# A Fourier mixing stage on one Trainium2 core: complex weights by three real products, transforms two steps ahead, inverses in one float32 pass

## The chip, the cores and the metric

The kernel runs on one core of a Trainium2 chip. The metric is the device time of one execution in microseconds (us); three executions of the kernel before took 1865.67, 1866.29 and 1866.52 us, median 1866.29. Lower is better.

## What is computed

Input `x` has 4 batches of 3072 rows and 256 columns. The reference transforms along the rows, mixes the 256 columns with a complex matrix, applies a soft threshold, transforms back, and feeds the result to two further blocks:

```
X = rfft(x, axis=1)
Yr = Xr @ w_r - Xi @ w_i + b_r
Yi = Xr @ w_i + Xi @ w_r + b_i
Y = soft_threshold(Yr, 0.01) + 1j * soft_threshold(Yi, 0.01)
y = irfft(Y)
x1 = moe(y)          # softplus/tanh gate between two matrices
out = moe2(x1)       # channel mix with a shift by one row
```

The change touches the first four lines and the inverse transform only. They are `part1` of the kernel, the first sixth of its time; `part2`, the two further blocks, is not touched.

## The kernel before, in words

`part1` splits the transform of length 3072 into small transforms of length 24, which VectorE does as additions and scaled additions on the tile `a` (4 MB, one per batch, two buffers), and products with 128x128 matrices, which TensorE does. The work is a loop `for u in range(48)`: 4 batches of 12 steps. `b, t = divmod(u, 12)`. Step u handles one residue class, in this order on TensorE:

- **F(u+1)**, `emit_F`: the forward transform of the next class, out of `a` and the plane `fm[t]`, into PSUM tile `xps`. It is a plain float32 product of 256 columns (4 products in the code, 8 matmul records in a trace).
- **M(u)**, `emit_M`: the complex mix into PSUM tile `yps`, which ScalarE has preloaded with the bias (`preload`). F's result is split by `post_F` into a rounded part `xh` (ScalarE copy to float32r) and a rest `xl` (VectorE subtraction), the weights into `wmh` and `wml`; three of the four products are taken. With [-wi | wr | wi] side by side in the weights, real and imaginary part each take one product of 512 columns: 3 terms x 2 halves of the contraction x 2 parts = 12 products of 512 columns. Steps with t = 0 hold two special rows and take 24 products of 256 columns.
- **I(u-1)**, `emit_I`: the inverse transform into PSUM tile `bps`. 13 steps do it as one plain float32 product with the plane `im`; the 35 steps in `SPLIT_I` do it as three products of float32r parts (`zh`, `zl` against the planes `imhi`, `imlo`), 12 products of 256 columns.

Around these, in the program order of the other engines: `post_M(u-1)` thresholds on ScalarE (`yb`), `post_I(u-2)` copies `bps` to `bs` and SyncE stores it to `b_dr`. VectorE's short transforms of later batches, and the length-24 back transforms `f3` on the tile `g`, are background work: a small planner (`Background`) keeps a clock of its own and fits them ahead of each `post_F` by the constants `SLACK` and by due steps.

Transfers run on queues that issue in order. SyncE's holds the loads of `a`, the stores to `b_dr` and `y_dr`, and the plain planes `im`. GpSimd's holds the split planes, and twice (u = 6 and u = 18) the helper `end_sum`, four calls (six transfers) that add thirds of `x` onto `a` in flight: the first pair waits for the load of lines 24 to 31, the second pair waits for the first. The planes go through a ring of 12 slots (`RING`, `stream`, `load_stream`), each 256 KB; a slot is refilled when the inverse that read it is done.

```
while sent < len(stream) and (sent < RING and u or sent >= RING and stream[sent - RING][0] <= u):
    load_stream(sent)
```

For batches 2 and 3 the tile `a` of two batches before is overwritten: lines 24 to 31 and 16 to 23 at t = 6, lines 8 to 15 and 0 to 7 at t = 10, each after the last F that reads them.

Of the kernel before, what the change touches and what calls it, by code (L numbers as in the profile page):

```python
# [11 lines left out]
F32 = mybir.dt.float32  # L12
F32R = mybir.dt.float32r
# [12 lines left out]
NB = 4  # L26
# [6 lines left out]
NT = 12  # L33
# [7 lines left out]
START = (18600, 20500)  # L41
SLACK = (2000, 3200, 600)

SUMS_AT = (11, 12, 23, 24)
LOWS_AT = 35
SPLIT_I = (*range(6, 10), *range(12, 22), *range(24, 34), *range(36, 47))
SPLIT_F = (45, 46)
TWO_PASS = range(42)
FIRST = tuple(u + 1 for u in SPLIT_I)
F3_PART1 = {(1, 2): [(0, 0)], (1, 8): [(0, 1)]}  # L50
# [129 lines left out]
def tile_fft_mix_moe_channel_mix(  # L180
# [30 lines left out]
    def tt(o, a, b, op):  # L211
        V.tensor_tensor(out=o, in0=a, in1=b, op=op)  # L212
# [4 lines left out]
    def act(o, i, f, **kw):  # L217
        S.activation(out=o, in_=i, func=f, **kw)  # L218
# [19 lines left out]
    def slot(dtype, name, k, i=None):  # L238
        if i is None:
            i = slots[0] % 24  # L240
            i += 8 * (8 <= i < 16) - 8 * (i >= 16)
            slots[0] += 1
            if i >= RING:
                i = RING + (i - RING + len(stream)) % RING
        return mat.tile([128, 512], dtype, tag="m%d" % (i % 24), name=name).rearrange("p (k f) -> p k f", k=k)

    RING = 12
    stream = []
# [24 lines left out]
    def priced(ops):  # L273
        return [(cost(256 * n), e) for op in ops for n, e in op]
# [417 lines left out]
    def part1():  # L692
        with ExitStack() as es:
# [18 lines left out]

            xt, ybt, ybs, xps, yps, bps, lows, flow, xsp, spare = {}, {}, {}, {}, {}, {}, {}, {}, {}, {}

# [33 lines left out]
            def post_F(u):  # L748
                t = u % NT
                ps = xps.pop(u)  # L750
                xh = xs_p.tile([128, 2, 256], F32R, tag="xh", name="xh")
                xl = xs_p.tile([128, 2, 256], F32R, tag="xl", name="xl")
                act(xh, ps, ACTF.Copy)
                tt(xl, ps, xh.bitcast(F32), SUB)
                xt[u] = (xh, xl)
                if t == 0:
                    zh, zl = (new_z(w).rearrange("p (h f) -> p h f", h=2) for w in ("zh", "zl"))
                    xt[u] += (zh, zl)
                    copy_z(u, 0)
                    if u == 0:  # L760
                        copy_z(u, 1)
# [7 lines left out]
            def preload(u):  # L769
                ps = yps[u] = psy.tile([128, 512], F32, tag="y", name="yps")  # L770
                act(ps, bias, ACTF.Copy)
                if u % NT == 0:
                    act(ps[0:1, 256:512], bias[0:1, 0:256], ACTF.Copy)

            def emit_M(u, part=None):
                t = u % NT
                ps = yps[u]
# [121 lines left out]
            for t in range(2, 4):  # L899
                nc.sync.dma_start(out=fm[t], in_=fsrc[:, t])  # L900
            for n in range(4):
# [3 lines left out]
            for n in range(4, SPLIT_I[0]):  # L905
                load_stream(n)
            sent = SPLIT_I[0]
            for i, v in enumerate((mu_k, mu_r)):
# [17 lines left out]
            bg.flush()  # L926
            m = split_mix(c1, mraw[0], 0) + split_mix(c1, mraw[1], 1)
            preload(0)
            post_F(0)
# [7 lines left out]
            bg.add(priced(tail[:7]), 5)  # L937
            bg.add(priced(tail[7:]), 8)
            NU = NB * NT
            mv[0] = ysrc = None  # L940
# [7 lines left out]
            pe, bg.clock = START  # L948
            x_at, y_at = bg.clock, 0.0
            for u in range(NU):  # L950
# [10 lines left out]
                if u == SUMS_AT[0] - 4:  # L961
# [12 lines left out]
                    emit(wq.load(u))  # L974
                bg.flush(u + 1)
                if u == 6:
                    S.activation(out=mu1, in_=mu, func=ACTF.Copy, scale=-1.0, bias=1.0)
                pe += (1450 if u + 1 in SPLIT_F else 1755) * (u + 1 < NU)
                if u + 1 < NU:
                    (emit_F3 if u + 1 in SPLIT_F else emit_F)(u + 1)  # L980
                if u:
# [31 lines left out]
                if u + 1 < NU:  # L1013
                    bg.until(pe + 700 + (0 if u == 0 else SLACK[2] if (u + 1) % NT == 0 else SLACK[1]) - sum(c for c, e in behind))
                    post_F(u + 1)
                    x_next = bg.spend(pe + 700, 602)
                if u >= SUMS_AT[0] - 3:
# [12 lines left out]
                pe = max(pe, x_at + 300) + (2720 if u else 900)  # L1030
                y_new = pe + 700
                if u:
                    emit_I(u - 1)
                    pe = max(pe, y_at + 300) + (1370 if u - 1 in SPLIT_I else 1755)
                x_at, y_at = x_next, y_new
# [571 lines left out]
```

## Time and profile before

| what | us or share |
|---|---|
| median of 3 runs | 1866.29 |
| profiled execution: its own time | 1866.71 |
| profiled execution: span from the first to the last instruction | 1864.9 |
| TensorE matmul busy | 1846.6 (99%) |
| TensorE weight load busy | 1596.3 (86%) |
| VectorE busy | 1404.7 (75%) |
| ScalarE busy | 1243.9 (67%) |
| mean granted TensorE clock | 0.997 |
| `part1` on TensorE: from the start to the last inverse | 0 to about 318 |

Shares are over the whole span. `part1` has its own limits, so it is read from its own stretch: which engine waits there, for what, and how long one step lasts on TensorE. A matmul's modelled end overlaps the next one's start, so the length of a group of products is taken from its start to the start of the next group.

### The profile page before, as it was taken

How to read it: one execution, taken by the hardware profiler on the slowest of the kernel's cores; microseconds unless marked ns; L12 is line 12 of the kernel's file. 1: busy time of each engine (PE TensorE's matmuls, PEld its weight loads, DVE VectorE, ACT ScalarE, POOL GpSimd, SP SyncE). 2: the span in 40 equal slices, each digit the busy share in tenths (PEclk: the TensorE clock that was granted, in tenths of full speed). 3: DMA queues.
4: the chain of work that ended last, by engine and by line, in shares of the span. 5: the costliest groups of instructions: out<-in, count | busy, mean ns of one | idle time of the engine just before them, and what ended most of it. 6: DMA issues, size and time to landing. Idle time of an engine off the chain costs nothing.

```text
span 1864.9 us, 27267 instructions
## 1 busy us (share of the span) xinstructions
PE 1846.6 (99%) x9798; PEld 1596.3 (86%) x9798; DVE 1404.7 (75%) x2494; ACT 1243.9 (67%) x2231; POOL 60.9 (3%) x103
## 2 busy tenths in 40 slices
PE   9998999999999999999999999999999999999999
PEld 7887888888888888888888888888999999999998
DVE  8896957998798879597777867666676666666654
ACT  4655588665667657575766757576877777777775
POOL 1212110000000000000000000000000000000000
PEclk9999999999999999999999999999999999999999
DMA  9969697545656554555646455452422222222211
GB/s 321 239 200 295 167 291 263 182 150 167 197 166 196 156 166 145 172 155 156 197 131 194 151 165 170 125 189 85 153 68 69 68 69 69 69 69 69 69 46 34
DMA packets 191509, 281.77 MB, mean 151 GB/s; under 512 B 17040, under 2 KB 106896, under 8 KB 191120
## 3 DMA queue, kind: packets, MB, share of 16 engines
q1 hardware_dynamic: 175360, 255.39, 43.3%
q0 software_dynamic: 14944, 23.60, 5.1%
q8 instruction: 78, 1.28, 0.3%
q10 hardware_dynamic: 1072, 1.05, 0.2%
q14 instruction: 55, 0.45, 0.1%
HBM read 203.43 MB, written 76.55 MB: 150 GB/s over the span
## 4 chain that ended last, share of the span: by engine, by line
PE 93%; DVE 3%; DMA 2%; issue 1%; SPq 0%; ACT 0%; POOL 0%; DVEq 0%; POOLq 0%; ACTq 0%
PE a L221 28%; PE x L221 16%; PE v L221 14%; PE c L221 11%; PE z L221 5%; PE d L221 5%; PE yps L221 5%; PE zps L221 4%; PE xps L221 3%; PE bps L221 3%; DMA a<-in_x_dram 1%; DMA y_dr<-g 1%; DVE a L212 1%; DVE g L212 1%; DMA imlo<-in_sel_dram 0%
## 5 line engine op out<-in xcount | busy, mean ns | idle before, releaser
L212 DVE TENSOR_TENSOR l<-k,h 128x512 fp32r<-128x512 f32 x576 | 391.7, 688 | 304.8 <-ACT k L218 150.6
L221 PE MATMUL a<-h,wo 128*128 128x512 f32 x1536 | 520.9, 389 | 0.0
L221 PEld LDWEIGHTS a<-h,wo 128*128 128x128 f32 x1536 | 288.3, 188 | 60.2
L221 PE MATMUL a<-l,wo 128*128 128x512 f32 x768 | 298.8, 389 | 0.0
L221 PE MATMUL v<-wv,h 128*128 128x256 f32 x1536 | 274.4, 278 | 0.0
L221 PEld LDWEIGHTS v<-wv,h 128*128 128x128 f32 x1536 | 244.4, 188 | 13.7
L218 ACT ACTIVATE k<-c 128x512 f32<-128x512 f32 x288 | 172.8, 600 | 108.4 <-PE c L221 96.2
L221 PE MATMUL x<-yc,wr 128*128 128x512 f32 x864 | 243.2, 390 | 0.0
L218 ACT ACTIVATE c<-x 128x512 f32<-128x512 f32 x288 | 169.5, 589 | 88.9 <-PE x L221 74.3
L218 ACT ACTIVATE k<-k 128x512 f32<-128x512 f32 x288 | 178.1, 633 | 65.9 <-DVE k L212 63.6
L221 PE MATMUL v<-wv,l 128*128 128x256 f32 x768 | 213.0, 277 | 0.0
L221 PEld LDWEIGHTS x<-yc,wr 128*128 128x128 f32 x864 | 161.9, 188 | 34.5 <-ACT d L218 0.4
L218 ACT ACTIVATE d<-x 128x512 f32<-128x512 f32 x144 | 84.6, 587 | 145.9 <-PE x L221 144.9
L221 PEld LDWEIGHTS a<-l,wo 128*128 128x128 f32 x768 | 144.1, 188 | 29.8
L221 PE MATMUL c<-yc,wr 128*128 128x512 f32 x576 | 161.8, 389 | 0.0
L221 PEld LDWEIGHTS v<-wv,l 128*128 128x128 f32 x768 | 144.4, 188 | 0.0
L218 ACT ACTIVATE h<-k 128x512 fp32r<-128x512 f32 x192 | 118.6, 629 | 30.2 <-DVE k L215 28.2
L212 DVE TENSOR_TENSOR k<-d,zs 128x512 f32<-128x512 f32 x144 | 98.8, 686 | 42.5 <-PE d L221 42.2
L221 PEld LDWEIGHTS c<-yc,wr 128*128 128x128 f32 x576 | 108.1, 188 | 22.6
L212 DVE TENSOR_TENSOR yc<-src,yc 128x512 fp32r<-128x512 f32 x168 | 112.0, 686 | 14.3 <-ACT yc L218 13.8
L221 PE MATMUL x<-yc,wk 128*128 128x512 f32 x432 | 122.5, 392 | 0.0
L212 DVE TENSOR_TENSOR g<-g 128x128 f32<-128x128 f32 (+3 forms) x264 | 111.1, 442 | 0.8
(122 smaller groups left out, 2896.5 us busy)
## 6 DMA issues: line engine op xcount, KB each, us to landing
wr<-h_dr SPq DMA_DIRECT2D x288, 256.0 KB, 2.7
b_dr<-bs SPq DMA_DIRECT2D x48, 256.0 KB, 4.6
src<-y_dr SPq DMA_DIRECT2D x24, 512.0 KB, 4.1
wr<-h_dr SPq DMA_DIRECT2D x96, 128.0 KB, 2.1
xk_dr<-tm SPq DMA_DIRECT2D x48, 256.0 KB, 3.1
xr_dr<-tm SPq DMA_DIRECT2D x48, 256.0 KB, 3.2
xr<-xr_dr SPq DMA_DIRECT2D x24, 512.0 KB, 3.8
src<-xk_dr SPq DMA_DIRECT2D x24, 512.0 KB, 4.3
```

The source lines that it names most:

```text
L212: V.tensor_tensor(out=o, in0=a, in1=b, op=op)
L218: S.activation(out=o, in_=i, func=f, **kw)
L221: T.matmul(out=o, lhsT=l, rhs=r, start=start, stop=stop, **kw)
```

## The change

It does five things.

1. **Three real products** for the 36 steps u = 9 to 47 with t > 0 (`gauss`). `post_F` also forms the sum of real and imaginary part (`xsf`: a ScalarE copy and a VectorE addition, both 128x256) and splits it (`xs`: one ScalarE copy, one VectorE subtraction). **G1(u+1)**, `emit_G1`, runs in step u: 6 products of 256 columns of that shared sum with wr, into one half of `yps`. `copy_G` has ScalarE copy this half into the other, in PSUM. **G2(u)**, `emit_G2`, then adds 13 products of 256 columns: one that adds the difference of the biases (`bo`), 12 with the weights wi - wr and -(wr + wi) (`wg`), which VectorE and ScalarE prepare once (`gauss_w`, `gauss_b`, due by step 9). `preload` copies 256 bias columns where it copied 512.
2. **All inverses plain**: `SPLIT_I` and `SPLIT_F` are empty. The planes `imhi`, `imlo`, `fmhi`, `fmlo` and the parts `zh`, `zl` of Y fall away.
3. **F two steps ahead** from step 8 on; step 7 does F(8) and F(9). Every third `xh`, `xl` pair lies in two former ring slots.
4. **The ring has 3 slots** and only `im` planes; from the fourth on they are issued by GpSimd. 10 plain planes that SyncE loaded move there.
5. The overwrite of `a` at t = 6 moves to t = 5 in batch 1, the one at t = 10 to t = 9 in both batches; the planner's costs and `SLACK` get new numbers.

```
-SLACK = (2000, 3200, 600)
+SLACK = (2000, 3200, 600, 1500)
+T_F, T_M, T_G1, T_G2, T_I = 1600, 2860, 730, 1690, 1725
-SPLIT_I = (*range(6, 10), *range(12, 22), *range(24, 34), *range(36, 47))
-SPLIT_F = (45, 46)
+SPLIT_I = ()
+SPLIT_F = ()
-FIRST = tuple(u + 1 for u in SPLIT_I)
+LEAD = 7
+FIRST = range(LEAD, NB * NT)
-    RING = 12
+    RING = (14, 16, 17)
...
+            gauss = lambda u: u > LEAD + 1 and u % NT
...
+                if gauss(u):
+                    act(xsf, ps[:, :, 0:128], ACTF.Copy)
+                    tt(xsf, ps[:, :, 128:256], xsf, ADD)
                 act(xh, ps, ACTF.Copy)
                 tt(xl, ps, xh.bitcast(F32), SUB)
                 xt[u] = (xh, xl)
+                if gauss(u):
+                    z = mat.tile([128, 512], F32R, tag="m%d" % (22 if u % 2 else 15), name="xs").rearrange(
+                        "p (s h f) -> p s h f", s=2, h=2)
+                    sh, sl = xsum[u] = z[:, 0], z[:, 1]
+                    act(sh, xsf, ACTF.Copy)
+                    tt(sl, xsf, sh.bitcast(F32), SUB)
...
+            def emit_G1(u):
+                ps = yps[u]
+                sh, sl = xsum.pop(u)
+                for k, (z, lo) in enumerate(((sh, 0), (sh, 1), (sl, 0))):
+                    for h in range(2):
+                        mm(ps[:, 0:256], z[:, h], wt["mix", h][lo][:, 256:512], False, k == 2 and h == 1, skip_group_check=True)
+
+            def copy_G(u):
+                act(yps[u][:, 256:512], yps[u][:, 0:256], ACTF.Copy)
+
+            def emit_G2(u):
+                ps = yps[u]
+                xs = xt.pop(u)
+                mm(ps[:, 256:512], ones, brow, False, False, skip_group_check=True)
+                for k, (zl, lo) in enumerate(((0, 0), (0, 1), (1, 0))):
+                    for h in range(2):
+                        for r in range(2):
+                            mm(ps[:, 256 - 256 * r:512 - 256 * r], xs[zl][:, h, 128 * r:128 * r + 128],
+                               wt["gauss", h][lo][:, 256 * r:256 * r + 256], False, k == 2 and h == 1, skip_group_check=True)
...
-                z = slot(F32 if kind == "im" else F32R, kind, 2, RING + n % RING)
+                z = slot(F32 if kind == "im" else F32R, kind, 2, RING[n % len(RING)])
-                    nc.sync.dma_start(out=z, in_=isrc[:, t])
+                    (nc.gpsimd if n >= len(RING) else nc.sync).dma_start(out=z, in_=isrc[:, t])
...
+                ahead = [v for v in ([u + 1] if u < LEAD else [u + 1, u + 2] if u == LEAD else [u + 2]) if v < NU]
...
+                if u + 1 < NU and gauss(u + 1):
+                    emit_G1(u + 1)
+                    copy_G(u + 1)
+                    pe = max(pe, x_at[u + 1] + 300) + T_G1
                 emit_M(u, None if u else 1)
...
-                if t == NT - 6 and b + 2 < NB:
+                if t == NT - 6 - b and b + 2 < NB:
...
-                if t == NT - 2 and b + 2 < NB:
+                if t == NT - 3 and b + 2 < NB:
...
-                while sent < len(stream) and (sent < RING and u or sent >= RING and stream[sent - RING][0] <= u):
+                while sent < len(stream) and stream[sent - len(RING)][0] <= u:
```

On TensorE, one step of batch 1 reads so before (`xps` is F, `yps` M, `bps` I; x4 counts the products of the code):

```order
L221 MATMUL xps<-fm,a 128x256 x4
L221 MATMUL yps<-wmh_261,xh 128x512 x2
L221 MATMUL yps<-wmh_266,xh 128x512 x2
L221 MATMUL yps<-wml_262,xh 128x512 x2
L221 MATMUL yps<-wml_267,xh 128x512 x2
L221 MATMUL yps<-wmh_261,xl 128x512 x2
L221 MATMUL yps<-wmh_266,xl 128x512 x2
L221 MATMUL bps<-imhi,zh 128x256 x4
L221 MATMUL bps<-imlo,zh 128x256 x4
L221 MATMUL bps<-imhi,zl 128x256 x4
```

and so in the change:

```order
L223 MATMUL xps<-fm,a 128x256 x4
L223 MATMUL yps<-wmh_255,xs 128x256
L223 MATMUL yps<-wmh_260,xs 128x256
L223 MATMUL yps<-wml_256,xs 128x256
L223 MATMUL yps<-wml_261,xs 128x256
L223 MATMUL yps<-wmh_255,xs 128x256
L223 MATMUL yps<-wmh_260,xs 128x256
L223 MATMUL yps<-bo 128x256
L223 MATMUL yps<-wg,xh 128x256 x8
L223 MATMUL yps<-wg,xl 128x256 x4
L223 MATMUL bps<-im,yb 128x256 x4
```

Twelve products of 512 columns became 6 + 13 of 256, and the six (G1) belong to the next step; the twelve products of the inverse became the four of the plain one.

On GpSimd's queue, around the first `end_sum` (the rows `a`), before; the plane `imlo_609` right behind it is read by I(12):

```order
L842 DMA imlo_422<-in_sel_dram 128x512
L842 DMA imhi_555<-in_sel_dram 128x512
L362 DMA a_165<-in_x_dram 128x4x256
L362 DMA a_165<-in_x_dram 128x2x256 x2
L362 DMA a_165<-in_x_dram 128x3x256
L362 DMA a_165<-in_x_dram 128x256
L362 DMA a_165<-in_x_dram 128x4x256
L842 DMA imlo_609<-in_sel_dram 128x512
```

and in the change, where `im_554` is the plane of I(7):

```order
L877 DMA im_554<-in_inv_dram 128x512
L362 DMA a_165<-in_x_dram 128x4x256
L362 DMA a_165<-in_x_dram 128x2x256 x2
L362 DMA a_165<-in_x_dram 128x3x256
L362 DMA a_165<-in_x_dram 128x256
L362 DMA a_165<-in_x_dram 128x4x256
L877 DMA im_606<-in_inv_dram 128x512
L877 DMA im_670<-in_inv_dram 128x512
```

The plane behind `end_sum` is now that of I(8), which TensorE reaches in step 9. At the second `end_sum` it is the plane of I(19), which TensorE reaches in step 20, three steps after the loads of that `end_sum` are issued.

On SyncE's queue, the overwrite of lines 8 to 15 and 0 to 7 of batch 0's tile stands so before:

```order
L612 DMA raw_695<-in_moe_w_in_dram 128x2x256 x2
L878 DMA b_dr0_57<-bs_740 128x2x256
L878 DMA b_dr0_57<-bs_802 128x2x256
L362 DMA a_165<-in_x_dram 128x6x256
L362 DMA a_165<-in_x_dram 128x2x256
L362 DMA a_165<-in_x_dram 128x4x256 x2
L878 DMA b_dr0_57<-bs_872 128x2x256
```

and so in the change:

```order
L612 DMA raw_695<-in_moe_w_in_dram 128x2x256 x2
L915 DMA b_dr0_57<-bs_734 128x2x256
L362 DMA a_165<-in_x_dram 128x6x256
L362 DMA a_165<-in_x_dram 128x2x256
L362 DMA a_165<-in_x_dram 128x4x256 x2
L915 DMA b_dr0_57<-bs_796 128x2x256
```

The four loads stand one store, that is one step, earlier.

## Rows read from the trace of the kernel before

**Rows 1.** Windows of the trace: us, then busy time of PE, PEld, DVE, ACT, POOL, clock, DMA.

```profile
100.00:150.00 50.00, 47.99 (x251) 41.76 (x252) 49.31 (x98) 26.65 (x47) 11.12 (x15) 0.97 0.72 201
...
266.00:272.00 6.00, 6.00 (x35) 5.27 (x33) 5.01 (x11) 5.91 (x12) 1.06 (x2) 1.00 1.00 318
```

**Rows 2.** Timeline of PE, one undisturbed step: start, us, instruction.

```profile
200.86 1.28 PE L221 MATMUL yps<-wmh,xh 128*128 128x512 f32 x4
...
203.81 0.64 PE L221 MATMUL bps<-imhi,zh 128*128 128x256 f32 x4
...
205.24 1.89 PE L221 MATMUL xps<-fm,a 128*128 128x256 f32 x8
```

**Rows 3.** Timeline of PE, the step with t = 0 and a plain inverse.

```profile
90.85 0.47 PE L221 MATMUL yps<-wmh,xh 128*128 128x256 f32 x1
...
93.91 1.89 PE L221 MATMUL bps<-im,yb 128*128 128x256 f32 x8
95.64 1.89 PE L221 MATMUL xps<-fm,a 128*128 128x256 f32 x8
```

**Rows 4.** Timeline of PE, a step whose F is split too.

```profile
294.00 0.64 PE L221 MATMUL xps<-fmhi,yc 128*128 128x256 f32 x4
...
295.44 1.09 PE L221 MATMUL yps<-wmh,xh 128*128 128x512 f32 x4
...
298.19 0.64 PE L221 MATMUL bps<-imhi,zh 128*128 128x256 f32 x4
```

**Rows 5.** Timeline of PE, steps 13 and 14, with what ended the idle time.

```profile
97.18 1.28 PE L221 MATMUL yps<-wmh,xh 128*128 128x512 f32 x4
...
104.11 0.75 PE L221 MATMUL bps<-imhi,zl 128*128 128x256 f32 x4 [2.01 <-DVE zl L212]
...
113.79 1.28 PE L221 MATMUL yps<-wmh,xh 128*128 128x512 f32 x4
```

**Rows 6.** Timeline of PE, step 25.

```profile
171.38 1.89 PE L221 MATMUL xps<-fm,a 128*128 128x256 f32 x8
...
182.35 2.07 PE L221 MATMUL yps<-wmh,xl 128*128 128x512 f32 x4 [6.90 <-DVE xl L212]
...
188.98 1.28 PE L221 MATMUL yps<-wmh,xh 128*128 128x512 f32 x4
```

**Rows 7.** Timeline of DVE ahead of those two places.

```profile
92.75 2.36 DVE L212 TENSOR_TENSOR a<-a 128x1024 f32<-128x1024 f32 x2 [5.30 <-DMA a<-in_x_dram]
...
99.19 0.68 DVE L212 TENSOR_TENSOR xl<-xps,xh 128x512 fp32r<-128x512 f32 x1
...
174.93 2.36 DVE L212 TENSOR_TENSOR a<-a 128x1024 f32<-128x1024 f32 x2 [2.32 <-DMA a<-in_x_dram]
```

**Rows 8.** Timeline of PE: F(7), F(8) and F(19).

```profile
54.06 1.89 PE L221 MATMUL xps<-fm,a 128*128 128x256 f32 x8
...
60.25 1.89 PE L221 MATMUL xps<-fm,a 128*128 128x256 f32 x8
...
130.03 1.89 PE L221 MATMUL xps<-fm,a 128*128 128x256 f32 x8
```

**Rows 9.** Timeline of POOL: the first plane behind each end_sum.

```profile
77.68 1.10 POOL L842 DMA_DIRECT2D imlo<-in_sel_dram  x1
...
149.76 1.10 POOL L842 DMA_DIRECT2D imhi<-in_sel_dram  x1
```

**Rows 10.** DMA view, the planes issued at 77.68 and 149.76: KB, us to landing.

```profile
imlo<-in_sel_dram POOLq DMA_DIRECT2D x1, 256.0 KB, 6.2
...
imhi<-in_sel_dram POOLq DMA_DIRECT2D x1, 256.0 KB, 11.0
```

**Rows 11.** Tile view of imhi, all 35 loads.

```profile
DMA to landing us min/median/max: 2.9/5.3/12.6
```

**Rows 12.** Timeline of ACT, two copies of 256 columns.

```profile
288.02 0.73 ACT L218 ACTIVATE wo<-q 128x256 fp32r<-128x256 f32 x2
288.64 0.60 ACT L218 ACTIVATE bs<-bps 128x512 f32<-128x512 f32 x1
```

More of the change, by code (lines that the diff above doesn't have):

```diff
@@ L242, in slot @@
             slots[0] += 1
-            if i >= RING:
-                i = RING + (i - RING + len(stream)) % RING
         return mat.tile([128, 512], dtype, tag="m%d" % (i % 24), name=name).rearrange("p (k f) -> p k f", k=k)
-    RING = 12
+    RING = (14, 16, 17)
     stream = []
@@ L711, in new_a @@
                 load_x(As[b], b)
-            xt, ybt, ybs, xps, yps, bps, lows, flow, xsp, spare = {}, {}, {}, {}, {}, {}, {}, {}, {}, {}
+            xt, xsum, ybt, ybs, xps, yps, bps, lows, flow, xsp, spare = {}, {}, {}, {}, {}, {}, {}, {}, {}, {}, {}
+            gauss = lambda u: u > LEAD + 1 and u % NT
             def emit_F(u):
@@ L750, in post_F @@
                 ps = xps.pop(u)
-                xh = xs_p.tile([128, 2, 256], F32R, tag="xh", name="xh")
-                xl = xs_p.tile([128, 2, 256], F32R, tag="xl", name="xl")
+                if u % 3:
+                    xh, xl = [xs_p.tile([128, 2, 256], F32R, tag=w, name=w) for w in ("xh", "xl")]
+                else:
+                    xh, xl = [slot(F32R, w, 2, i) for w, i in (("xh", 12), ("xl", 13))]
+                if gauss(u):
+                    act(xsf, ps[:, :, 0:128], ACTF.Copy)
+                    tt(xsf, ps[:, :, 128:256], xsf, ADD)
                 act(xh, ps, ACTF.Copy)
@@ L770, in preload @@
                 ps = yps[u] = psy.tile([128, 512], F32, tag="y", name="yps")
+                if gauss(u):
+                    act(ps[:, 0:256], bias[:, 0:256], ACTF.Copy)
+                    return
                 act(ps, bias, ACTF.Copy)
@@ L773, in preload @@
                     act(ps[0:1, 256:512], bias[0:1, 0:256], ACTF.Copy)
+            def emit_G1(u):
[15 more added lines that the diff above has]
+                               wt["gauss", h][lo][:, 256 * r:256 * r + 256], False, k == 2 and h == 1, skip_group_check=True)
             def emit_M(u, part=None):
+                if gauss(u):
+                    return emit_G2(u)
                 t = u % NT
@@ L900, in part1 @@
                 nc.sync.dma_start(out=fm[t], in_=fsrc[:, t])
-            for n in range(4):
+            for n in range(len(RING)):
                 load_stream(n)
@@ L904, in part1 @@
                 nc.sync.dma_start(out=fm[t], in_=fsrc[:, t])
-            for n in range(4, SPLIT_I[0]):
-                load_stream(n)
-            sent = SPLIT_I[0]
+            sent = len(RING)
             for i, v in enumerate((mu_k, mu_r)):
@@ L927, in part1, with gauss_w, low, gauss_b @@
             m = split_mix(c1, mraw[0], 0) + split_mix(c1, mraw[1], 1)
+            xsf = c1.tile([128, 2, 128], F32, name="xsf")
+            for h in range(2):
+                wt["gauss", h] = [mat.tile([128, 512], F32R, tag="m%d" % (18 + 2 * h + k), name="wg") for k in range(2)]
+            bo = mat.tile([128, 512], F32R, tag="m23", name="bo")
+            brow, ones = bo[:, 0:256], bo[:, 256:384]
+            def gauss_w(h):
+                q = pools["st"].tile([128, 512], F32, tag="q", name="q", bufs=3)
+                hi, lo = wt["gauss", h]
+                wr, wi = mraw[h][:, 0, :], mraw[h][:, 1, :]
+                def low():
+                    act(hi, q, ACTF.Copy)
+                    tt(lo, q, hi.bitcast(F32), SUB)
+                return [(420.0, lambda: tt(q[:, 0:256], wi, wr, SUB)),
+                        (420.0, lambda: stt(q[:, 256:512], wr, -1.0, wi, MULT, SUB)), (700.0, low)]
+            def gauss_b():
+                q = pools["st"].tile([128, 512], F32, tag="q", name="q", bufs=3)
+                def low():
+                    act(brow, q[:, 0:256], ACTF.Copy)
+                    act(ones, fm[1][:, 0, 0:128], ACTF.Copy, scale=0.0, bias=1.0 / 64)
+                    tt(brow[64:128], q[64:128, 0:256], brow[64:128].bitcast(F32), SUB)
+                return [(420.0, lambda: tt(q[:, 0:256], bias[:, 256:512], bias[:, 0:256], SUB)), (420.0, low)]
             preload(0)
@@ L938, in part1 @@
             bg.add(priced(tail[7:]), 8)
+            bg.add(gauss_w(0) + gauss_w(1) + gauss_b(), LEAD + 2)
             NU = NB * NT
@@ L948, in part1 @@
             pe, bg.clock = START
-            x_at, y_at = bg.clock, 0.0
+            x_at, y_at = {0: bg.clock}, 0.0
             for u in range(NU):
@@ L974, in part1 @@
                     emit(wq.load(u))
-                bg.flush(u + 1)
+                ahead = [v for v in ([u + 1] if u < LEAD else [u + 1, u + 2] if u == LEAD else [u + 2]) if v < NU]
+                bg.flush(max(ahead, default=u))
                 if u == 6:
                     S.activation(out=mu1, in_=mu, func=ACTF.Copy, scale=-1.0, bias=1.0)
-                pe += (1450 if u + 1 in SPLIT_F else 1755) * (u + 1 < NU)
-                if u + 1 < NU:
-                    (emit_F3 if u + 1 in SPLIT_F else emit_F)(u + 1)
+                f_end = []
+                for v in ahead:
+                    emit_F(v)
+                    pe += T_F
+                    f_end.append(pe)
                 if u:
@@ L1012, in part1 @@
                     behind = wq.vec(u, 4)
[L1013 to L1016, printed above, removed]
+                for v, e in zip(ahead, f_end):
+                    bg.until(e + 700 + (0 if u == 0 else SLACK[2] if v % NT == 0 else SLACK[3] if gauss(v) else SLACK[1]) - sum(c for c, e in behind))
+                    post_F(v)
+                    x_at[v] = bg.spend(e + 700, 602)
+                    if gauss(v):
+                        x_at[v] = bg.spend(e + 1300, 900)
                 if u >= SUMS_AT[0] - 3:
@@ L1029, in part1 @@
                     copy_z(u + 1, 1)
-                pe = max(pe, x_at + 300) + (2720 if u else 900)
+                pe = pe + T_G2 if gauss(u) else max(pe, x_at[u] + 300) + (T_M if u else 900)
                 y_new = pe + 700
@@ L1033, in part1 @@
                     emit_I(u - 1)
-                    pe = max(pe, y_at + 300) + (1370 if u - 1 in SPLIT_I else 1755)
-                x_at, y_at = x_next, y_new
+                    pe = max(pe, y_at + 300) + T_I
+                y_at = y_new
                 if u + NT in SPLIT_F:
```

## The prediction

> **What bounds the kernel now.** I first cut the trace into windows [rows 1]. TensorE is filled nearly everywhere; the clock in 100 to 150 us is 0.97, so something stops TensorE there. The waits of TensorE in `part1` lead to two places. In step 13 an inverse waits 2.01 us for VectorE's `zl` [rows 5]; in step 25 a mix waits 6.90 us for VectorE's `xl` [rows 6]. VectorE's timeline tells why: it works in order, and both times an addition on `a` stands ahead of the split and waits for a load of `x` [rows 7]. Everywhere else a step lasts what its products last, so `part1` is bound by TensorE's products plus those two stalls, and each product that goes, goes from the end time.
>
> The lengths of a step's parts come from the PE timeline, start to start. Twelve products of 512 columns after a plain F take 203.81 - 200.86 = 2.95 us, the split inverse 205.24 - 203.81 = 1.43 [rows 2]. After a split F the same twelve take 298.19 - 295.44 = 2.75 [rows 4], so the switch from a plain product costs 0.20. The 24 products of 256 columns with t = 0 take 93.91 - 90.85 = 3.06, less the switch 2.86, or 0.119 each; a plain inverse takes 1.73 [rows 3], a plain F 97.18 - 95.64 = 1.54 [rows 3, 5], a split F 1.44 [rows 4]. An undisturbed step is 1.54 + 2.95 + 1.43 = 5.92.
>
> **The change part by part.**
>
> *Three products.* G1 and G2 are 19 products of 256 columns: 19 x 0.119 + 0.20 = 2.46 where 2.95 stood, 0.49 less. In 33 of the 36 steps that is 16.2 us. In steps 44 and 45 F was split, so M took 2.75 and F now costs 0.10 more: 0.19 gained each. Step 47 gains about 0.1. Together **-16.7**.
>
> *Plain inverses.* 1.73 for 1.43, 35 times: **+10.5**. On TensorE the net is **-6.2**, and the step becomes 1.54 + 2.46 + 1.73 = 5.73.
>
> *The old stalls.* From 97.18 to 113.79 two steps took 16.61 us, 4.77 over two of 5.92 [rows 5]. From 171.38 to 188.98, F and one step took 17.60, 10.14 over 7.46 [rows 6]. The excess is the wait and a slower stretch behind it: four products of `xl` show 2.07 us in their row where the clock had dropped [rows 6]. The loads VectorE waited for are now issued one step earlier, and F runs a step further ahead, so a late `xl` has one more step, 5.73 us, before TensorE needs it. Against the first stall (2.01 us of wait) that is ample. Against the second (6.90) the earlier load and the extra step together make 11. I take both as gone: **-14.9**; bounds -8 and -14.9, should a half of the second remain.
>
> *The ring of three.* This is a new wait. A plane is now loaded two steps ahead, no longer five or more, and it stands behind `end_sum` on GpSimd's queue, whose second pair can't be issued until the first has landed. First place, I(8): nothing up to step 6 is changed ahead of it, so `end_sum` and the plane behind it should be issued as before, at 77.68 [rows 9], and that plane landed 6.2 us later [rows 10]: 83.9. TensorE starts F(8) at 60.25 [rows 8] and then does F(8) and F(9) 3.08, M(7) 2.95, I(6) 1.73; F(10) 1.54, G1(9) 0.91, M(8) 2.75, I(7) 1.73; F(11) 1.54, G1(10) 0.91, G2(9) 1.55; 18.7 in all, and stands at I(8) at 78.9. The wait is 5.0. The four loads of lines 0 to 15 now start at about F(11)'s end, 76.5, beside that transfer; I add 1.0 (bounds 0 and 4). Behind a stall the slower stretch costs 10.14 - 6.90 = 3.2 or 4.77 - 2.01 = 2.8, with small waits in both; I take 2.4. First place: 8.4.
>
> Second place, I(19): F(19) ended at 130.03 + 1.54 = 131.57 [rows 8], the plane behind the second `end_sum` was issued at 149.76 [rows 9], 18.2 later, and landed after 11.0 [rows 10]: 29.2 after F(19). In the change TensorE stands at I(19) 0.91 + 1.55 + 1.73, two steps of 5.73, and 1.54 + 2.46 after F(19)'s end: 19.65. With 11.0 the wait is 9.5; with the 6.2 of the first place 4.7. The 11.0 had four more planes behind it and the stores of `y_dr` beside it; the planes are gone and F(19) now stands a step ahead of those stores, so I stay near the low end: 5.5, plus 2.4 for the clock: 7.9. Both places: **+16.3**, bounds +9.7 (4.7 + 5.0, no loss of clock) and +24.
>
> A rule of the Trainium skill (DMA: Bandwidth & Descriptors, section on the anatomy of one DMA on the gpsimd path) gives a transfer issued by GpSimd about 2.0 us plus its bytes over 436 GB/s, for 256 KB an estimate of 2.6. The fastest of 35 planes took 2.9, the median 5.3 [rows 11], so rule and row agree on an idle queue only. By the rule the plane of I(8) would land at 80.3, 1.4 late, and that of I(19) 1.1 late, and the sum below would be -6.2 - 14.9 + 2.5 = -18.6.
>
> *What I cost at nothing.* VectorE: per step one subtraction of 512 columns (0.68, [rows 7]) goes, an addition and a subtraction of 256 come; if each costs over half, the step grows by a little, at most by 0.68. It was busy 49.31 of 50 us from 100 to 150 [rows 1], and the nine operations of `gauss_w` and `gauss_b` come on top, at most 9 x 0.68 = 6.1. Its cover is the step of lead and the stall at I(8), during which it runs on; without them up to 4 us come out on TensorE. ScalarE: two copies of 512 columns go (0.60 each, the length of `bs` in [rows 12]), four of 256 come at 0.31 from start to start [rows 12]: level. While it decodes weights it was busy 5.91 of 6.00 [rows 1], and TensorE's step is now 5.73: some 0.25 short in eight steps, 2 us in all, hidden as long as the lead of a step lasts (bounds 0 and 2). `copy_G` stands ahead of the next bias copy and threshold and waits for G1, which ends a G2 before the threshold's own source does: nothing. SyncE loses 10 planes: nothing.
>
> **The sum.** -6.2 - 14.9 + 16.3 = **-4.8**. The profiled execution took 1866.7 by itself, 0.4 over the median of the runs: 1861.9 for such a one, **1861.5** beside the median 1866.3. The end of `part2` is bound by its own products and moves along.
>
> **The rivals.**
>
> *The planes come in time* (33%). Fewer planes are in flight, so `end_sum` is through earlier, or the plane passes as fast as the fastest of the 35, in 2.9 [rows 11]; it would then be 1.6 late at I(8) and 1.4 at I(19), too short for me to add a loss of clock. The Trainium skill's rule above leads the same way. For it: 35 transfers of 256 KB are gone from the queues. Against it: GpSimd issued the second pair only when the first had landed, and nothing among those transfers was in flight then. Time: -6.2 - 14.9 + 3.0 = -18.1; VectorE's cover is thinner then, so up to 4 come back: -14.1 to -18.1, about 1850.
>
> *The ring starves* (12%, slower). A slot is free when I(u-1) ends, the plane is wanted two steps less one inverse later: 11.46 - 1.73 = 9.7, of which the issue takes about 0.5. A plane that needs 11.0 is 1.8 late, one that needs 12.6 is 3.4 late [rows 11]. For it: such landings happened, in the stretch with the stores of `y_dr` and the loads of `x`. Against it: they came with up to five planes queued behind `end_sum`, and the median is 5.3. At 1.8 each, five late planes eat the gain; eight of them give -4.8 + 14.4 = +9.6, about 1876.
>
> *The sum product is late* (5%, no change). G1 needs `xs`, whose chain is ScalarE, VectorE, ScalarE, VectorE in a queue that is 99% busy. If it is late by 0.14 us in each of 36 steps, the 4.8 are gone: 1866. Against it: the chain has a whole step.
>
> **How the numbers follow.** The forecast has 50%: 1857 to 1867 by its bounds. A measurement of this kernel tells about 0.2% or 3.7 us from no change, so faster begins below 1862.6; the forecast lies barely beyond, and I give it two thirds of its 50% as faster (33%) and 17% as same. The rival with planes in time adds 32% to faster and 1% to same, the late sum 5% to same, the starving ring 12% to slower. The range 1849 to 1868 holds the forecast, most of the first rival and the third.
>
> **What would show it.** Right: F, G and I of a step at 5.73; no wait for `xl` at steps 13 and 25; two waits of TensorE on a transfer of `im`, of 4 to 9 us, at I(8) near 79 us and at I(19), each with a lower clock behind it; `part1` shorter by some 5 us. Wrong: no such waits and `part1` shorter by 15 or more; waits on `im` at many other steps; TensorE waiting for `xs` or for `copy_G`; 19 products that take more than 2.6 us.

## The result: 0.54% slower, and the profile after

The changed kernel took 1874.67, 1875.46, 1876.30 and 1877.16 us, median 1875.88; the kernel before took 1865.98 in the same comparison. The ratio is 1.0054, 95% interval [1.0037, 1.0072]: slower. The profiled execution took 1874.67 by itself, with a span of 1872.9, against 1866.71 and 1864.9 before. The forecast was 1861.5, with a range of 1849 to 1868: wrong, in size and in sign.

The first product of `part2` starts at 325.79 us, before at 317.94. That is 7.85 of the 8.0 us, so the whole loss lies in `part1`, and the chain forecast there can be followed term by term. First the PE timeline of one undisturbed step, which answers to [rows 2]:

```profile
105.29 1.89 PE L223 MATMUL xps<-fm,a 128*128 128x256 f32 x8
106.83 0.59 PE L223 MATMUL yps<-wmh,xs 128*128 128x256 f32 x2
...
107.72 0.28 PE L223 MATMUL yps<-bo 128*128 128x256 f32 x1
...
109.28 1.89 PE L223 MATMUL bps<-im,yb 128*128 128x256 f32 x8
111.01 0.81 PE L223 MATMUL xps<-fm,a 128*128 128x256 f32 x3
```

F 1.54, G1 0.89, G2 1.56, I 1.73: 5.72 where 5.73 was forecast. Next the waits of TensorE from 50 to 326 us (engine, line, what for; us in total, times, longest):

```profile
PE yps L223 <- ACT yps L220: 9.3, 13, 1.8
PE bps L223 <- DMA im<-in_inv_dram: 5.5, 2, 2.9
PE bps L223 <- DVE yb L217: 2.1, 3, 1.0
PE xps L223 <- DVE xl L214: 2.1, 2, 1.2
```

The two old stalls of [rows 5, 6], on `zl` at step 13 and on `xl` at step 25, are gone. The two waits for a plane of `im` came where they were forecast, at I(8) and I(19), but shorter (2.62 and 2.88). New are 13 waits of G1 for `yps`, which ScalarE preloads; the forecast has none. Here is the largest pair of neighbours, first on PE:

```profile
128.69 1.89 PE L223 MATMUL xps<-fm,a 128*128 128x256 f32 x8
131.28 0.51 PE L223 MATMUL yps<-wmh,xs 128*128 128x256 f32 x2 [0.70 <-ACT yps L220]
...
135.39 1.89 PE L223 MATMUL xps<-fm,a 128*128 128x256 f32 x8
138.62 0.51 PE L223 MATMUL yps<-wmh,xs 128*128 128x256 f32 x2 [1.34 <-ACT yps L220]
```

then on ACT,

```profile
129.75 0.60 ACT L220 ACTIVATE xh<-xps 128x512 fp32r<-128x512 f32 x1 [3.27 <-DVE xsf L214]
130.24 0.41 ACT L220 ACTIVATE xs<-xsf 128x256 fp32r<-128x256 f32 x1
130.55 0.38 ACT L220 ACTIVATE yps<-yps 128x256 f32<-128x256 f32 x1
130.85 0.37 ACT L220 ACTIVATE yps<-bias 128x256 f32<-128x256 f32 x1
```

and on DVE:

```profile
129.30 0.42 DVE L214 TENSOR_TENSOR xsf<-xps,xsf 128x256 f32<-128x256 f32 x1
130.38 0.69 DVE L214 TENSOR_TENSOR xl<-xps,xh 128x512 fp32r<-128x512 f32 x1 [0.66 <-ACT xh L220]
130.99 0.41 DVE L214 TENSOR_TENSOR xs<-xsf,xs 128x256 fp32r<-128x256 f32 x1
131.32 5.40 DVE L214 TENSOR_TENSOR g<-g 128x1024 f32<-128x1024 f32 x10
136.64 0.42 DVE L214 TENSOR_TENSOR xsf<-xps,xsf 128x256 f32<-128x256 f32 x1
```

Read from the bottom. From one addition `xsf` to the next VectorE needs 136.64 - 129.30 = 7.34 us, which is just the length of TensorE's step there. It idles for 0.66 of that, between the addition and `xl`, since `xl` needs ScalarE's `xh`; and ScalarE's `xh` had itself waited 3.27 for VectorE's addition. `xh` needs nothing of the sum. But both read the PSUM tile `xps`, and here two readers of one tile on different engines ran one after the other, in the order in which the program has them: the addition first. The Trainium skill (PSUM — Partial Sum Buffer, section "PSUM bank collisions raise a hardware error") states that two engines must not be in one PSUM bank at once, reads against reads included, and that the compiler's scheduler orders such accesses. The waits here agree with an ordering; no run here shows what reads at the same time would do.

The waits of DVE and of ACT from 50 to 326 us say how often:

```profile
DVE xl L214 <- ACT xh L220: 24.2, 37, 0.7
```

```profile
ACT xh L220 <- DVE xsf L214: 70.6, 36, 5.3
```

The account of `part1`, from F's start to the next F's start in both profiled executions:

| term | forecast | measured |
|---|---|---|
| products and inverses | -6.2 | -6.2 (steps of 5.72 or 5.73) |
| old stalls | -14.9 | -14.9 (no such wait) |
| ring of three: steps of 9.14, 5.97, 10.30, 6.56 for 5.73, 4.89, 5.73, 5.73 | +16.3 | +9.9 |
| late sum: steps 17 to 21 +3.8, 29 to 34 +4.4, 36 +3.7 | 0 | +11.9 |
| ScalarE in steps 43 to 45: 5.86, 6.64, 6.64 for 5.73 (xh_first below still has 5.80, 6.59, 6.59) | 0 | +2.0 |
| F(8) to F(10): 10.48 for 3.08 + 2.95 + 1.73 | 0 | +2.7 |
| F(7) starts at 54.43, not 54.06 | 0 | +0.4 |
| the rest, by subtraction; in it the last three inverses, which wait 2.1 for `yb` | 0 | +2.0 |
| sum | -4.8 | +7.8 |

### The profile page after: what moved, and what is told of

It reads as the page before. It is cut to its first block, busy times and chain, and to the rows that moved or that the text cites. A ratio compares the mean times of both kernels' runs of the same rounds, so it can differ in the third digit from the quotient of the medians.

```text
span 1872.9 us, 27574 instructions
## 1 busy us (share of the span) xinstructions
PE 1846.2 (99%) x9902; PEld 1600.6 (85%) x9902; DVE 1413.5 (75%) x2537; ACT 1247.7 (67%) x2306; POOL 46.0 (2%) x74
## 4 chain that ended last, share of the span: by engine, by line
PE 87%; DVE 5%; ACT 3%; DMA 3%; issue 1%; POOL 0%; SPq 0%; DVEq 0%; POOLq 0%; ACTq 0%
PE a L223 28%; PE x L223 16%; PE v L223 14%; PE c L223 10%; PE z L223 5%; PE d L223 5%; PE zps L223 4%; DMA a<-in_x_dram 2%; PE yps L223 2%; PE xps L223 1%; PE bps L223 1%; DVE a L214 1%; DMA im<-in_inv_dram 1%; ACT xh L220 1%; DVE g L214 1%
```

## The experiments

Three theories. A: VectorE is the short engine, and the 0.66 us that it idles in each step make the sum late. B: ScalarE's order is the trouble, the bias copy stands behind copies that wait. C: the ring is the loss, and the waits for `yps` are its wake.

**no_sum**: the shared product left out.

```
-            gauss = lambda u: u > LEAD + 1 and u % NT
+            gauss = lambda u: False
-            bg.add(gauss_w(0) + gauss_w(1) + gauss_b(), LEAD + 2)
```

> Edit: no shared product: all steps keep their twelve products of 512 columns and gauss_w, gauss_b, xsf, sh, sl and copy_G are not issued; plain inverses, F two steps ahead and the ring of three stay. Theory A or B (the sum's chain through ScalarE and VectorE causes the waits for yps): those waits are gone, a step is 1.54 + 2.95 + 1.73 = 6.22 us, 36 x 0.49 = 17.2 us of products come back against 14.7 us of waits and 2 to 3 at steps 9 and 10, the ring's waits shrink by 1 to 2 us as TensorE comes later: 1872 to 1876. Theory C (the waits for yps come from running F two steps ahead or from the ring): waits of the same size stay, and the time is 1876 + 17 = 1890 or more.

1876.31 us, ratio to the kernel before 1.0050 [1.0038, 1.0063], and no wait for `yps`. C is out: with two waits for `im` (10.6 us in all) there is no wait for `yps`. As it stands, the shared product earns nothing: it makes a step 0.46 us shorter (5.73 for 6.19) and loses as much by what comes late. The ring's waits had been expected to shrink by 1 to 2 us; they grew from 5.5, so the two kernels differ in more than the product.

**xh_first**: ScalarE's `xh` ahead of the addition.

```
                 if gauss(u):
                     act(xsf, ps[:, :, 0:128], ACTF.Copy)
-                    tt(xsf, ps[:, :, 128:256], xsf, ADD)
                 act(xh, ps, ACTF.Copy)
+                if gauss(u):
+                    tt(xsf, ps[:, :, 128:256], xsf, ADD)
                 tt(xl, ps, xh.bitcast(F32), SUB)
```

> Edit: in post_F ScalarE's copy xh is issued before VectorE's addition xsf, so it no longer waits for it; nothing is left out. Theory A (VectorE is the short engine in the busy stretches, and the chain ScalarE, VectorE, ScalarE, VectorE makes it idle 0.66 us in every step between the addition and xl, 24.2 us in 37 waits): VectorE's idle before xl falls below 5 us, TensorE's 9.3 us of waits for yps falls to 3 or less, and the kernel gains 0.5 to 0.66 us in some 18 steps, 9 to 12 us: about 1865. Theory B (ScalarE's order is the trouble: the bias copy and copy_G stand behind sh, which still waits for the addition): TensorE's waits stay at 8 to 10 us, and the time stays within 2 us of 1875.9. Theory C (the loss is the ring's): the same as B.

1865.87 us, 10.0 less than the change; against the kernel before 0.9999 [0.9990, 1.0008]. The DVE timeline of a step now shows the three without a gap, and the wait list of TensorE has shrunk:

```profile
115.74 0.42 DVE L214 TENSOR_TENSOR xsf<-xps,xsf 128x256 f32<-128x256 f32 x1
116.07 0.68 DVE L214 TENSOR_TENSOR xl<-xps,xh 128x512 fp32r<-128x512 f32 x1
116.67 0.42 DVE L214 TENSOR_TENSOR xs<-xsf,xs 128x256 fp32r<-128x256 f32 x1
117.00 0.42 DVE L214 TENSOR_TENSOR a<-a 128x256 f32<-128x256 f32 x1
```

```profile
PE bps L223 <- DMA im<-in_inv_dram: 5.6, 1, 5.6
PE bps L223 <- ACT yb L220: 2.8, 1, 2.8
...
PE yps L223 <- ACT yps L220: 1.2, 2, 0.6
```

The group takes VectorE 117.00 - 115.74 = 1.26 where it took 131.32 - 129.30 = 2.02. The second line is I(8), at 84.87, where it stood at 84.90 in the change; its `yb` was done at 78.0, so what it waits for is the plane again, issued at 75.39 and 9.5 us to landing. ScalarE's copy `xs` still waits for the addition (50.8 us in 36 waits), so B's order is still there, and TensorE hardly waits for it. The ring's waits grew as the others went: I(19) now waits 5.63, and the four steps around I(8) and I(19) cost 13.1 us over undisturbed ones, which is nearer to the 16.3 forecast. In the change the late sum had held TensorE back until the plane of I(19) was nearly there.

**xl_twice**: the former, and the same subtraction once more, as a load on VectorE.

```
                 tt(xl, ps, xh.bitcast(F32), SUB)
+                if gauss(u):
+                    tt(xl, ps, xh.bitcast(F32), SUB)
```

> Edit to the kernel with xh first: the subtraction that makes xl is issued twice in each of the 36 steps, with the same result, which gives VectorE 0.6 us of work in the place of the 0.66 us of idle time that the swap had taken away. Theory A (it was VectorE's time that was short): the waits for yps come back in the same steps as in the changed kernel, 8 us or more, and the time is 1872 to 1877. Theory B' (the swap helped because ScalarE was no longer blocked): the time stays at 1865 to 1868.

1877.72 us, 1.0061 [1.0048, 1.0075], 0.7 above what theory A gave. The steps of the change come back one by one:

| step F(u) | 16 | 17 | 18 | 19 | 20 | 21 |
|---|---|---|---|---|---|---|
| change | 5.73 | 6.09 | 5.86 | 6.70 | 7.34 | 6.50 |
| xh_first | 5.73 | 5.72 | 5.73 | 5.73 | 5.72 | 5.73 |
| xl_twice | 5.72 | 6.17 | 5.85 | 6.65 | 7.31 | 6.48 |

So it is VectorE's time that counts, idle or at work.

**bias_first**: the change, with `copy_G` and the bias copy ahead on ScalarE (their old places further down are taken out).

```
+                if u + 1 < NU and gauss(u + 1):
+                    emit_G1(u + 1)
+                    copy_G(u + 1)
+                if u + 2 < NU:
+                    preload(u + 2)
                 for v, e in zip(ahead, f_end):
                     bg.until(
```

> Edit to the changed kernel: ScalarE does copy_G and the next bias copy ahead of the copies of post_F in place of behind them; the wait of xh for the addition stays, nothing is left out. Theory A (VectorE is the short engine; G1 would only wait for its sum xs in place of the bias copy): the waits of TensorE at G1 stay, named after VectorE or ScalarE, 8 to 12 us, and the time is 1873 to 1878. Theory B (the bias copy is late because it stands behind xh and sh in ScalarE's order): the waits for yps fall below 2 us and the time to about 1862 to 1866.

1880.41 us, 1.0080 [1.0066, 1.0093]. That is 2.4 above what theory A gave, and far from B. The waits of TensorE stay, 15 where there were 13, and get another name, that of the sum's own copy:

```profile
PE yps L223 <- ACT xs L220: 10.6, 15, 1.6
```

B is out. The bias copy was only the last of two things that hang on the addition.

**charge**: the planner's price for the addition and second subtraction.

```
-                        x_at[v] = bg.spend(e + 1300, 900)
+                        x_at[v] = bg.spend(e + 1300, 1450)
```

> Edit: the planner charges VectorE 1450 ns in place of 900 for the addition and the second subtraction of a step, so less background work is put ahead of the following splits; the operations are the same. In the trace one step's four operations take VectorE 2.0 us from start to end where 602 + 900 = 1.5 is charged. Theory A (VectorE falls 0.5 us behind the planner's clock in every step and is late through that): the additions start earlier after F, TensorE's waits for yps halve, 5 us gained, about 1871; not all, since the work put off has due dates. Theory B (ScalarE's order alone) and theory C (the ring): within 2 us of 1875.9.

1884.17 us, 1.0094 [1.0080, 1.0108]: a miss, 8 us more in place of 5 less. In the stretch of the table above it did what was expected (steps 17 to 21 in 5.72 to 6.13), but the work it put off came due later, and the waits for `im` grew from 5.5 to 8.8 us. PE and DVE, where F(44) starts 7.55 us late; the trace names no releaser, but the scaled additions on `a` stand just there:

```profile
295.57 2.90 PE L223 MATMUL xps<-fm,a 128*128 128x256 f32 x6 [7.55 <-issue]
```

```profile
294.25 2.35 DVE L217 SCALAR_TENSOR_TENSOR a<-a 128x1024 f32<-128x1024 f32 x2
```

Putting work off makes no time on a short engine. The price of 602 + 900 ns was right for the work; what it missed was the gap, which the swap removes.

**plane_first**: the plane of `im` ahead of `end_sum` (the loop of `load_stream` moved ahead of the overwrite of `a`).

```
+                while sent < len(stream) and stream[sent - len(RING)][0] <= u:
+                    load_stream(sent)
+                    sent += 1
                 if t == NT - 6 - b and b + 2 < NB:
```

> Edit: GpSimd issues the step's plane of im before end_sum in place of behind it. The two waits for im (2.62 and 2.88 us, with slower clocks behind them: steps of 9.14, 5.97 and 10.30 us in place of 5.73, 4.9 and 5.73) go in every theory. Theory A (VectorE is short of time): the two stalls are also VectorE's cover, so part of the 9 us comes back as waits for yps right behind them, which grow from 9.3 to 12 us: 4 to 6 us gained, about 1871. Theory C (the ring is the whole loss, the waits for yps are its wake): 9 us gained and the waits for yps behind 160 us shrink too, 1866 or less. Theory D (the plane is late only by the queue, and end_sum, now behind a plane's own wait, makes VectorE late instead): TensorE waits for xl at steps 13 or 25 again, no gain.

1871.03 us, 1.0026 [1.0018, 1.0035], 4.9 less than the change. The waits for `im` are gone, those for `yps` rose from 9.3 to 14.6 us in 16 waits, more than the 12 expected: half of the gain came back, as theory A had it.

**no_sum_plane**: no_sum with that edit.

> Edit: no shared product (as no_sum) and the plane of im ahead of end_sum: what is left of the change is F two steps ahead and plain inverses. If the terms hold by themselves (plain inverses +10.5, the two old stalls -14.9, no ring waits): 4.4 us below the kernel before, 1862, with steps of 6.19 throughout; from no_sum it is its 1876.3 less the 16.9 us by which its steps around I(8) and I(19) (14.06, 6.53, 12.91, 7.33) exceed the others (6.19, and 5.36 with t = 0): 1860. If end_sum behind the plane makes VectorE's loads late: waits for xl, 1866 or more.

1865.62 us, 0.9996 [0.9987, 1.0005], against an expected 1860 to 1862. TensorE still waits 3.1 us for `im` once, at I(9), whose plane is now the first behind `end_sum`: issued at 77.54, it is there at 87.65. The two steps there take 9.59 and 7.01 for 5.36 and 6.19, 5.0 us more. Without these it would be 1860.6, where the terms +10.5 and -14.9 give 1861.4, so the two hold together; the edit moves the first late plane on by one step, and that is not far enough where nothing else holds TensorE up.

**both**: xh_first and plane_first together.

> Edit: xh first and the plane of im ahead of end_sum. In the kernel with xh first the steps around I(8) and I(19) take 13.1 us more than the undisturbed ones (10.24, 5.11, 13.34, 6.48 for 5.73, 4.89, 5.73, 5.73). Theory A with VectorE now having time enough: all 13 go, 1853. Theory A with VectorE just short of time (these stalls were its cover): 3 to 5 of them come back as waits for yps in steps 15 to 23, 1856 to 1858. Theory D (end_sum, behind the plane's wait, now makes the loads late): waits for xl or zl at steps 13 and 25, 1860 or more.

1856.33 us, 0.9948 [0.9935, 0.9960]. That is in the range of the second branch, but not by its mechanism: TensorE waits for `yps` only 1.2 us in all. What is left of the ring is a wait for a plane, 1.83 us, in the step that begins with F(23), which takes 7.79. It is the plane of I(20), now the first behind the second `end_sum`, as I(9)'s is behind the first. I(9) comes at 87.70, just behind its plane (issued at 77.04, 10.1 to landing), since F(8) to F(10) hold TensorE up before. VectorE's time now suffices without the stalls as cover.

**both_due**: the weights of the sum due later.

```
-            bg.add(gauss_w(0) + gauss_w(1) + gauss_b(), LEAD + 2)
+            bg.add(gauss_w(0) + gauss_w(1) + gauss_b(), LEAD + 4)
```

> Edit: as the former, and the weights of the shared product (gauss_w, gauss_b) are due at step 11 in place of 9. If TensorE's two waits for xl at F(9) and F(10), 2.1 us, and the slower start of those steps come from the nine operations put ahead of the splits of steps 8 and 9 on VectorE, these waits go and 2 to 3 us are gained on the former: about 1850. If F(8) and F(9), issued together with two buffers of xps, are the cause by themselves, nothing changes.

1854.21 us, 0.9941 [0.9928, 0.9953]. The two waits for `xl` are still there (2.1 us) and F(8) to F(10) takes 10.50. But this run tests nothing: the later due step moved no operation. DVE's last operation on the weights, in both and then here:

```profile
52.03 0.69 DVE L214 TENSOR_TENSOR wg<-q,wg 128x512 fp32r<-128x512 f32 x1 [1.20 <-ACT wg L220]
```

```profile
51.12 0.69 DVE L214 TENSOR_TENSOR wg<-q,wg 128x512 fp32r<-128x512 f32 x1 [1.20 <-ACT wg L220]
```

All of this trace lies about 1 us ahead (F(7) at 54.19 for 55.31), and VectorE, like ScalarE and GpSimd, has the same operations in the same order. So the operations on the weights are not cleared, and no_sum speaks against them: it leaves them out, and F(8) to F(10) takes 7.95 there, with no wait for `xl`. The 2.1 us between the medians of both and both_due show how far two measurements of the same order of work can lie apart.

**both_slack**: both, with the short slack around step 8.

```
-SLACK[3] if gauss(v) else SLACK[1]
+SLACK[3] if gauss(v) or v >= LEAD else SLACK[1]
```

> Edit to the kernel with xh first and the plane ahead: the splits of steps 7 to 9 and of all later ones that come ahead of another F get the planner's short slack (1500 ns in place of 3200). In that kernel TensorE waits 1.04 and 0.88 us for xl at F(9) and F(10), since VectorE splits step 7 six us after its F with background additions ahead, and xps has two buffers. If that order is the cause, both waits go and 2 to 3 us are gained: 1853 to 1854; if the background work there has due dates that force it, nothing changes: 1856.

1855.05 us, 0.9949 [0.9935, 0.9962]. The waits for `xl` are gone and F(8) to F(10) takes 8.04 in place of 10.30, but the next step takes 7.67 for 7.02, and that of F(12) 6.30 for 4.89, with a wait of 1.15 us for `yps`. What TensorE no longer waits for at F it partly waits for later; a gain cannot be told from none.

**both_slack_sh**: the former, with `sh` behind `bs` on ScalarE in steps 35 to 42.

```
+                for v in ahead:
+                    if gauss(v) and LOWS_AT <= u < LOWS_AT + 8:
+                        split_sum(v)
```

> Edit to the former: in steps 35 to 42 ScalarE copies sh behind the inverse's copy bs in place of ahead of it, so it does not idle 0.49 us for the addition. In the kernel with xh first and the plane ahead, ScalarE has no other idle time in steps of 6.60 at 270 to 283 us (two of them, 0.87 over 5.73). If ScalarE is the bound there: these steps shrink to 6.1, 1 us gained on the former. If the chain through VectorE is: nothing.

1852.74 us, 0.9928 [0.9915, 0.9940]. The two steps of 6.60 and 6.59 became 5.72 and 5.73: with weights to decode ScalarE was the bound there, and it idled for the addition, as these rows of ACT in the kernel both show (it has no other idle time in the step):

```profile
270.38 0.42 ACT L220 ACTIVATE xs<-xsf 128x256 fp32r<-128x256 f32 x1 [0.49 <-DVE xsf L214]
270.70 0.58 ACT L220 ACTIVATE bs<-bps 128x512 f32<-128x512 f32 x1
```

ScalarE's own step, from one copy `xsf` to the next, went from 275.63 - 269.03 = 6.60 to 275.09 - 268.99 = 6.10, just this idle time. TensorE's fell further, to 5.72, since ScalarE now comes to these steps less behind: 3.8 us after F(44) starts (275.09 - 271.28) it copies that F's `xsf`, where it was 6.2 (275.63 - 269.41), and the lead covers the rest. The edit also moves VectorE's subtraction `xs` behind work on the weights, so ScalarE's order is not all that it changes. As a time the gain is not clear of what both and both_due differ by.

**sum_split**: the former, with the second pair of `end_sum` one step later, behind the next plane.

```
-                    end_sum(A, b + 2)
+                    end_sum(A, b + 2, 1)
...
+                if t == NT - 5 - b and b + 2 < NB:
+                    end_sum(As[b + 2], b + 2, 2)
```

> Edit to the former (xh first, plane ahead, short slack, sh behind bs): the second pair of end_sum's transfers is issued one step later, behind the next plane of im. In the former TensorE still waits 2.95 us at I(19), and that step takes 10.49 us in place of 5.73: its plane stood behind the second pair, was issued at 144.29 and landed at 153.8. If its place in GpSimd's queue is the cause, wait and slow step go, 4.8 us: 1848. If the landing is slow because of the other transfers of that time, the wait stays: 1851 to 1853. If the later sum makes VectorE late: waits for xl or zl at steps 13 and 25, over 1853.

1850.39 us, 0.9917 [0.9904, 0.9931]: faster than both kernels, 16.1 us below the kernel before and some 25 below the change. The waits of TensorE that are left from 50 to 345 us:

```profile
PE yps L223 <- ACT yps L220: 2.1, 4, 1.1
PE bps L223 <- DVE yb L217: 1.7, 2, 1.0
PE xps L223 <- DVE xl L214: 0.2, 1, 0.2
```

None is for `im`, and the granted clock is 1.000 over the span. The step that took 10.49, from F(23) to F(24), takes 5.72. It is that of I(20); the expectation calls it I(19). POOL issues that plane at 144.29 in the former, behind the second pair, and here ahead of it:

```profile
144.29 1.67 POOL L879 DMA_DIRECT2D im<-in_inv_dram  x2
```

```profile
135.44 0.76 POOL L877 DMA_DIRECT2D im<-in_inv_dram  x1
```

It still needs 7.8 us to land, so it was the plane's place in GpSimd's queue, and not a faster transfer. The median fell by 2.4 us, half of the 4.8 expected, and that by itself is no more than both and both_due differ by; the step in question had taken 7.54 in both_slack, so its cost was not the same in each execution.

## Why the prediction was wrong

- **Products and inverses, -6.2**: right. 19 products in 0.89 + 1.56 = 2.45 for a forecast 2.46, the plain inverse 1.73.
- **Old stalls, -14.9**: right, no such wait in the change; no_sum_plane bears out both terms together.
- **The ring, +16.3**: right in place and kind. In the change it cost 9.9, since TensorE came 3.4 us later to I(8) than reckoned; in xh_first, where little else is late, 13.1, and I(19)'s wait was 5.63 for 5.5, and behind the two waits 1.9 and 2.7 us were lost where 2.4 each was forecast. That the plane of I(8) came at the forecast 83.9 + 1.0 = 84.9 was luck: it was issued at 75.84 in place of 77.68 and needed 9 us to land in place of 7.2. The rival that the ring starves gave the measured total by a mechanism that did not occur: no other step waits for `im`.
- **"What I cost at nothing"**: this step failed. For VectorE I compared busy time with busy time ("the step grows by a little, at most by 0.68") and named as cover the step of lead. The four operations of `post_F` follow one another across two engines, and the program's order put 0.66 us of idle time between them. VectorE had been busy 49.31 of 50 us before [rows 1]. In the change it is busy only 42.84 from 100 to 150 us, with 4.6 us of these gaps beside that, and its chain still made steps of up to 7.34: the busy share did not show it. The lead of one step was used up: in the rows above the addition for F(18) starts at 129.30, when F(19) is already running.
- **"`copy_G` ... nothing"** was right by itself: the wait has the name of `yps`, but bias_first shows that the place of these copies in the order was not the cause.
- **The rival "the sum product is late"** was the case, at +11.9 in place of the +4.8 that I gave it, and 5% was too little. It was weighed against "the chain has a whole step" and not worked out as a chain with its waits. By the Trainium skill (PSUM — Partial Sum Buffer, the section named above) such a wait was to be expected from the diff alone: the addition stands in it between two ScalarE reads of the same `ps`. The trace agrees, with the 36 waits of `xh` above.
- **ScalarE, "hidden as long as the lead of a step lasts"**: wrong in two steps of 0.9 (both_slack_sh), +2.0 with step 43, at the upper end of its bounds of 0 to 2. The 0.25 a step does not follow from its row: 5.91 of 6.00 in a step of 5.92 is 5.83, 0.10 over 5.73. What counted was the 0.49 that ScalarE idles for the addition.
- **F(8) and F(9) in one step, +2.7**: not seen. `xps` has two buffers, and F(9) waits 1.23 us for `xl` of step 7, which VectorE does at 63.00 with additions on `a` ahead; both_slack, which reorders them, takes this wait away. The operations for the weights of the sum seem to push them there: VectorE does eight (the forecast counted nine) from 46.74 to 53.31, 2.4 us of it idle for ScalarE, and in no_sum, without them, that `xl` is at 61.15 and nothing waits for it. No run moved them alone.
- **"1857 to 1867 by its bounds"** does not come out of the bounds given: -6.2 - 14.9 + 9.7 is -11.4, or 1854.9, and -6.2 - 8 + 24 is +9.8, or 1876. The range was too narrow for its own terms, though the loss came by another.

Open: how the rest of 2.0 us is made up, and why a plane behind a part of `end_sum` needs 7.5 to 10.1 us to land where the median of the change's planes is 3.3. Neither was tried by itself.

## What to carry to other kernels

Price a new piece of work on a busy engine from the start of its first operation to the start of what follows, waits between engines included, and not by the sum of its operations. Two readers of one PSUM tile on different engines ran in program order here, so put first the one that other work hangs on: one swapped line was worth 10 us, where putting work off by the planner's price lost 8. And a stall hides others: the ring's waits were 5.5 us with the late sum and 8.4 without it, so fixes are to be measured together. Last, look in the trace whether an edit moved anything before reading a result out of it: one here did not.

## What the runs showed of the hardware that was not expected

What TensorE lost by a wait was not always the wait alone. Behind the wait of 1.34 us at 138.62 the two products take 0.51 as behind that of 0.70 at 131.28: nothing more was lost. Behind a wait of 2.62 at 84.90 the eight records of an inverse take 2.57 us, behind 2.88 at 156.88 they take 2.85, in place of 1.89 in an undisturbed step; in the PE timeline of the change:

```profile
84.90 2.57 PE L223 MATMUL bps<-im,yb 128*128 128x256 f32 x8 [2.62 <-DMA im<-in_inv_dram]
...
156.88 2.85 PE L223 MATMUL bps<-im,yb 128*128 128x256 f32 x8 [2.88 <-DMA im<-in_inv_dram]
```

and in that of xh_first, behind 5.63 us:

```profile
155.18 3.75 PE L223 MATMUL bps<-im,yb 128*128 128x256 f32 x8 [5.63 <-DMA im<-in_inv_dram]
```

The granted clock says the same. In xh_first it is 0.50 from 155.18 to 158.70, the level of 1.2 GHz; in the change it is 1.00 (2.4 GHz) from 100 to 150 us, where waits of up to 1.34 lie, and 0.76 from 84.90 to 87.26, 0.50 from there to 89.00. But the length of a wait does not tell it alone. These are the wait at step 36 of the change, the inverse a little later, and a wait of the same length in both:

```profile
241.88 0.50 PE L223 MATMUL yps<-wmh,xs 128*128 128x256 f32 x2 [1.84 <-ACT yps L220]
...
245.12 2.60 PE L223 MATMUL bps<-im,yb 128*128 128x256 f32 x8
```

```profile
153.49 1.97 PE L223 MATMUL bps<-im,yb 128*128 128x256 f32 x8 [1.83 <-DMA im<-in_inv_dram]
```

Behind the first the clock is 0.64 from 242.80 to 247.56, and the step takes 8.57 for 4.89; behind the second it is 1.00 from 153.49 to 155.29, and the step takes 7.79 for 5.73. No run here shows what makes the difference.
